# Block-sparse attention and a gated MLP on one core: chunk masks by product for the last four head pairs, and batch 0's query halves on GpSimd

## The chip, the cores and the metric

One core of a Trainium2 chip runs one program. The metric is device time of one execution in microseconds. A core has TensorE (PE; its weight loads are listed as PEld), VectorE (DVE), ScalarE (ACT), GpSimd (POOL) and SyncE (SP), each with an instruction queue of its own that is worked in order, and 16 DMA engines that the queues of SyncE and, for six loads at the start, ScalarE feed.

## What is computed

Attention with a selection of chunks, then a gated MLP. There are 4 batches, 8 heads, 768 positions, 64 elements per head; a chunk has 32 positions, so there are 24 of them.

```python
k_min, k_max = k_chunks.min(axis=3), k_chunks.max(axis=3)
ub = np.sum(np.maximum(q[:, :, :, None, :] * k_min[:, :, None, :, :],
                       q[:, :, :, None, :] * k_max[:, :, None, :, :]), axis=-1)
ub = np.where(causal, ub, -1e9)                      # by chunk
top_chunks = np.argsort(ub, axis=-1)[..., -6:]
scores = scale * q @ k.T
mask = sel & (pos[:, None] >= pos[None, :])          # chosen chunks, and causal
attn = softmax(np.where(mask, scores, -1e9))
x = (attn @ v)                                       # to [3072 tokens, 512]
h = x @ w_in                                         # 512 -> 2048
out = (h * np.clip(h + 3, 0, 6) / 6) @ w_out         # 2048 -> 512
```

The first six chunks of positions (192 rows of queries, `Q0`) select all that causality leaves them, so a mask is needed for the other 576 (`NQ`, twice `HQ` = 288) only.

## The kernel before

**Units of work.** Two heads of a batch are a *pair*; there are 16, and batch b has pairs 4b to 4b+3. The score matrix of a pair is kept transposed (keys on partitions, queries along the free dimension) and cut to its causal part in six *units* u (`UNITS`, line 23): blocks of up to 512 columns for both heads, 2688 columns per head in all. The MLP works on *groups* g of 384 tokens, two for each batch.

**The order is written by hand.** `ORDER` (line 34) is a list of tokens such as `S.12.4.a`: operation, pair and unit, PSUM place. The last lines (690 to 692) run down the list and issue each token's instructions to its engine. Within an engine the instructions stand in that order; between engines they wait for data and for buffers. PSUM has three double banks `a`, `b`, `c` (tiles PBa, PBb, PBc) and two single ones `x`, `y` (PSx, PSy).

What the tokens mean:

- `LK LQ LV AK AQ` load half a pair's K, Q, V for one head (SP, or ACT for the two with A); `lk lq lv` load pairs 4 to 15, K and Q turned in blocks of 32 by the access pattern, and `kd qd` finish the turning on DVE. `wl wc` load and cast weights.
- Batch 0 (pairs 0 to 3): `KT QT` transpose on PE in halves; `KB QB` cast to bf16 on ACT (lines 402, 405); `MX MN` chunk maxima and minima on DVE; `RP`, `RN` or `RA` the positive and negative part of Q (lines 419, 423, 427); `UH` the bounds on PE; `UB TH T8 SE LH MT` bias, transpose, top 8, comparison, transpose back and copy of the mask.
- Pairs 4 to 15: `mx mn kx rp` the same preparation; `ud us tr tm se tb` bounds of two pairs at once on PE (line 490), bias, 32x32 block transpose, top 8, comparison and transpose back on DVE (lines 495 to 512); `mv` copies the mask into spare rows of the query tile on POOL (line 314); `kc qc` cast K and Q (POOL, ACT).
- `S` scores on PE, `ex` exp on ACT into PT, `af` the causal triangle of a diagonal block on POOL (line 555). `A B` weighted values on PE, `na nb` division by the sum and storing to XB on DVE.
- XB is transposed for the MLP into XT by `X`/`xe` (PE, then a copy on DVE; lines 604, 608) or by `xt` (three DMA transposes on SP; line 597). `H` hidden matmuls (line 615, 1 token = 2x4 matmuls of 384 columns), `hu gt` the gate on ACT and DVE (lines 623, 626), `O` output projection (line 653, 4 matmuls of 512 columns a token), `ot st` scaling on ACT and the store on SP.

**Scores and masks before.** Pairs 0 to 3 score with both heads' 64 rows side by side in the array (line 537) and add a mask term by further matmuls (line 542). Pairs 4 to 15 (line 530) put 32 rows of mask and a fixed spreading matrix beside the 64 rows of K and Q in one matmul of 96 or 128 rows, so that a chunk that is not chosen gets -8192 before exp; the two heads follow one another.

## Time and profile before

| | |
|---|---|
| time, median of 3 runs | 270.98 us (270.34 to 271.39) |
| profiled execution | 270.87 us, span 268.9 us |
| DVE, ACT, POOL busy | 179.4, 184.1, 123.3 us |
| granted TensorE clock | 0.999 |
| DMA | 35.94 MB, mean 134 GB/s |
| longest waits, in total | POOL (`af`) for ACT's exp 50.0 us; DVE (`gt`) for ACT's `hu` 33.5 us |

The page gives busy time by engine, the chain of work that ended last, groups of instructions by source line, and DMA issues. The trace also gives each engine's instructions in order of time, merged where neighbours are alike, with the idle time ahead of them and what ended it in brackets. "96*128 96x384" of a matmul is the size of its weights and of the streamed operand.

### The profile page before, as it was taken

Reading aid. Unit: us, or ns where it says so; the run is one execution under the profiler, and the core shown is the slowest. Engines: PE = TensorE matmul, PEld = TensorE weight load, DVE = VectorE, ACT = ScalarE, POOL = GpSimd, SP = SyncE. Lnnn points to the kernel's source line nnn. Section 1 sums busy time; section 2 is a strip of 40 time slices with the busy share of each in tenths; the row PEclk is TensorE's granted clock in tenths of the full one; section 3 lists DMA queues with packets and bytes.
Section 4 is the critical chain, followed back from the end, with each engine's and each line's share of the span. In section 5 each row is a group of like instructions: output and inputs, shape, how many; then the busy total and the mean of one; then the engine's idle time right before and its main releaser. Section 6 shows DMA issues by size and latency. Waiting matters only on the chain.

```text
span 268.9 us, 6552 instructions
## 1 busy us (share of the span) xinstructions
PE 256.6 (95%) x2492; PEld 156.0 (58%) x2492; DVE 179.4 (67%) x430; ACT 184.1 (68%) x251; POOL 123.3 (46%) x234
## 2 busy tenths in 40 slices
PE   3998989999999999999999999999999999999995
PEld 1665777655455568655555655655555666555544
DVE  2698897889596889988897488746792314632420
ACT  1568899476689898494986588876668796423432
POOL 6901899676857895083392214850325521000000
PEclk9999999999999999999999999999999999999999
DMA  8979895789999928979667437512420021221023
GB/s 167 195 165 169 161 338 111 280 225 324 230 185 194 221 65 143 211 152 204 99 156 160 97 82 174 95 25 58 124 57 2 0 61 41 46 93 39 0 78 117
DMA packets 129102, 35.94 MB, mean 134 GB/s; under 512 B 121776, under 2 KB 122032, under 8 KB 129072
## 3 DMA queue, kind: packets, MB, share of 16 engines
q1 hardware_dynamic: 126672, 34.94, 56.7%
q10 hardware_dynamic: 2400, 0.59, 1.2%
q8 instruction: 19, 0.31, 0.5%
q14 instruction: 11, 0.09, 0.1%
HBM read 27.26 MB, written 6.29 MB: 125 GB/s over the span
## 4 chain that ended last, share of the span: by engine, by line
PE 78%; DVE 6%; ACT 6%; DMA 4%; SPq 2%; issue 2%; POOL 1%; DVEq 0%; ACTq 0%
PE PSx L653 15%; PE PBc L615 11%; PE PBb L615 9%; PE PSy L653 8%; PE PBa L615 8%; PE PBa L530 4%; PE PBb L530 3%; ACT PT L548 3%; PE PBc L530 3%; PE PBa L653 3%; PE PSy L571 2%; PE PSx L571 2%; DMA KSM<-in_k_dram 2%; DMA XT<-XB 2%; ACT U L623 1%
## 5 line engine op out<-in xcount | busy, mean ns | idle before, releaser
L615 PEld LDWEIGHTS <-WIN 128*128 128x128 bf16 x512 | 49.2, 98 | 34.6 <-issue 1.0
L555 POOL TENSOR_SCALAR_AFFINE_SELECT PT<-PT 128x256 bf16<-128x256 bf16 x96 | 37.2, 411 | 52.5 <-ACT PT L548 50.0
L653 PEld LDWEIGHTS <-GT 128*128 128x128 bf16 x368 | 34.7, 97 | 36.2 <-issue 1.5
L653 PE MATMUL PSx<-WOUT,GT 128*128 128x512 bf16 x208 | 51.4, 379 | 0.0
L615 PE MATMUL PBc<-XT,WIN 128*128 128x384 bf16 x200 | 36.6, 326 | 0.3 <-ACT PT L548 0.2
L548 ACT ACTIVATE PT<-PBa 128x1024 bf16<-128x1024 f32 (+2 forms) x35 | 32.2, 919 | 5.9 <-PE PBa L530 5.2
L548 ACT ACTIVATE PT<-PBb 128x1024 bf16<-128x1024 f32 (+2 forms) x32 | 29.3, 916 | 5.3 <-PE PBb L530 4.4
L626 DVE SCALAR_TENSOR_TENSOR GT<-U,PBc 128x768 bf16<-128x768 bf16 x25 | 23.6, 946 | 12.0 <-ACT U L623 11.8
L623 ACT ACTIVATE U<-PBc 128x768 bf16<-128x768 f32 x25 | 20.2, 809 | 16.0 <-PE PBc L615 14.5
L548 ACT ACTIVATE PT<-PBc 128x1024 bf16<-128x1024 f32 (+2 forms) x29 | 27.2, 937 | 5.3 <-PE PBc L530 4.6
L530 PEld LDWEIGHTS <-KB 96*128 96x128 bf16 x240 | 21.4, 98 | 15.5 <-issue 1.6
L615 PE MATMUL PBb<-XT,WIN 128*128 128x384 bf16 x160 | 29.3, 326 | 0.6 <-DMA XT<-XB 0.6
L653 PE MATMUL PSy<-WOUT,GT 128*128 128x512 bf16 x112 | 28.1, 379 | 0.0
L615 PE MATMUL PBa<-XT,WIN 128*128 128x384 bf16 x152 | 27.8, 326 | 0.0
L626 DVE SCALAR_TENSOR_TENSOR GT<-U,PBb 128x768 bf16<-128x768 bf16 x20 | 19.0, 950 | 11.3 <-ACT U L623 11.1
L314 POOL COPY QB<-MTM 32x288 bf16<-32x288 bf16 x48 | 20.2, 421 | 12.9 <-DVE MTM L512 8.3
L571 PEld LDWEIGHTS <-PT 128*128 128x128 bf16 x672 | 23.8, 97 | 3.0 <-issue 0.2
L626 DVE SCALAR_TENSOR_TENSOR GT<-U,PBa 128x768 bf16<-128x768 bf16 x19 | 18.0, 945 | 10.6 <-ACT U L623 10.6
L623 ACT ACTIVATE U<-PBa 128x768 bf16<-128x768 f32 x19 | 15.3, 807 | 13.5 <-PE PBa L615 13.5
L623 ACT ACTIVATE U<-PBb 128x768 bf16<-128x768 f32 x20 | 16.2, 810 | 12.2 <-PE PBb L615 12.0
L362 DVE TENSOR_REDUCE KM<-KSM 128x24 f32<-128x768 f32 x24 | 22.2, 942 | 0.2
L306 POOL CAST KB<-KSM 64x768 bf16<-64x768 f32 x24 | 19.7, 827 | 5.6 <-issue 3.1
(193 smaller groups left out, 385.3 us busy)
## 6 DMA issues: line engine op xcount, KB each, us to landing
out_dram<-OT SPq DMA_DIRECT2D x23, 256.0 KB, 2.4
...
WS<-in_moe_w_in_dram SPq DMA_DIRECT2D x4, 1024.0 KB, 7.7
WS<-in_moe_w_out_dram SPq DMA_DIRECT2D x4, 1024.0 KB, 6.2
...
```

The source lines that it names most:

```text
L306: engine.tensor_copy(T, src[i % 3][rows])
L314: nc.gpsimd.tensor_copy(aug(QB, i, e)[g:g + CH, Q0 + HQ * h:Q0 + HQ * (h + 1)], MTD[(d // 2) % 2][src:src + CH, e])
L362: nc.vector.tensor_reduce(out=KM[i % 4][:, m, 0:NCH], in_=k_turned(i).rearrange("p (c w) -> p c w", w=CH), axis=AX.X, op=(A.max, A.min)[m] ...
L530: nc.tensor.matmul(PSB[c][:, e, at:at + n], lhsT=K[rows, j * P:(j + 1) * P], rhs=Q[rows, q0:q0 + n], start=True, stop=True)
L548: nc.scalar.activation(PT[i % 3][u][:, :, 0:n], PSB[slot["S", i, u]][:, :, 0:n], ACT.Exp, scale=float(scale))
L555: nc.gpsimd.affine_select(out=T[:, :, lo:lo + P], in_=T[:, :, lo:lo + P], pattern=[[0, 2], [1, P]], compare_op=A.is_ge, fill=0.0, base=0, ...
L571: nc.tensor.matmul(O[:, e, t, :], lhsT=PT[i % 3][u][:, e, lo:lo + P], rhs=VB[i % 4][:, j, e, :], start=(j == 0), stop=(j == qb))
L615: nc.tensor.matmul(PSB[c][:, ff, 0:GRP], lhsT=WIN[:, kt, (2 * f + ff) * P:(2 * f + ff + 1) * P], rhs=XT[g % 3][:, kt, :], start=(kt == 0), ...
L623: nc.scalar.activation(slot["R", g, f][:], PSB[slot["H", g, f]][:, :, 0:GRP], ACT.Relu, bias=3.0)
L626: nc.vector.scalar_tensor_tensor(out=GT[g % 2][:, 2 * f:2 * f + 2, :], in0=slot["R", g, f][:], scalar=6.0, in1=PSB[slot["H", g, f]][:, :, ...
L653: nc.tensor.matmul(PSS[c], lhsT=GT[g % 2][:, f, t * P:(t + 1) * P], rhs=WOUT[:, f, :], start=(f == 0), stop=(f == FT - 1))
```

## The change

For pairs 12 to 15 (`PRODUCT`, the pairs with an `sm` token) the scores are made as in pairs 0 to 3, the two heads in two 64-row tiles, without a mask term. The comparison gives 1 for a chosen chunk. `sm` writes the mask of a pair to a DRAM tile, each of its 32 chunk rows four times; `ml` reads for one key block j the four chunks' rows back, each onto 32 partitions; `am` clears the triangle of the diagonal block in it, and `mu` multiplies PT by it behind exp. The masks lie in the weight staging tiles WS and in two new tiles MX5, which hold the identity and the spreading matrix of batch 0 earlier. `mv` falls away for these pairs, `kc` and `qc` cast all 128 rows at once, and `af` stays for the units of the first 192 queries alone.

For batch 0 ACT copies a half of Q once to SBUF (`QF`), and POOL makes the bf16 cast (`QC`) and the positive part (`PP`) from there, in place of ACT's `QB` and `RP`. Group 2 uses `xt` in place of `X` and `xe`. The whole list `ORDER` is another one. Number of tokens, before and after: `QB` 8 to 0, `RP` 8 to 0, `QF` `QC` `PP` 0 to 8 each; `X` `xe` 6 to 4 each, `xt` 5 to 6; `af` 80 to 68, `mv` 24 to 16, `kc` and `qc` 24 to 20 each; `sm` 0 to 4, `ml` `mu` 0 to 24 each, `am` 0 to 16; all others keep their number.

The list's first lines, and its lines from pair 12's bounds to the first hidden group of batch 3, then the functions:

```diff
+LK.0.1.0 AK.0.0.1 LQ.0.1.1 LQ.0.1.0 LK.0.0.0 PRP AK.1.0.1 LQ.0.0.0 LK.1.0.0 AQ.0.0.1 LK.2.0.0 LK.0.1.1 LQ.1.0.0 PRI
+AK.2.0.1 PRD Z.b.4 PRL EG.0 QT.0.1.y EG.2 KT.0.0.x MN.0.0 MX.0.0 KT.1.0.b MX.1.0 MN.1.0 QT.0.0.a RN.0.0 EG.3
+LK.1.1.1 KT.0.1.c AQ.2.0.1 LQ.2.0.0 AQ.1.0.1 KB.0.0 KT.2.0.x QF.0.1 PP.0.1 QC.0.1 LK.3.0.1 LK.1.1.0 QF.0.0 KB.1.0
+RA.0.1 PP.0.0 MX.2.0 UH.0.0.a MN.2.0 UB.0.0 LV.1.0.1 LK.3.0.0 QT.2.0.y TH.0.0.b LQ.1.1.0 QC.0.0 KB.2.0 MN.0.1
+LK.2.1.1 MX.0.1 EG.1 QF.2.0 T8.0.0 RN.2.0 LQ.1.1.1 QC.2.0 PP.2.0 QT.1.0.x QF.1.0 QC.1.0 PP.1.0 KB.0.1 UH.0.1.a
+UB.0.1 UH.2.0.c KT.3.0.y UB.2.0 SE.0.0 RN.1.0 KT.1.1.a KB.1.1 MX.3.0 LQ.3.0.0 LK.3.1.1 MN.3.0 TH.0.1.c T8.0.1
+LQ.2.1.1 QT.1.1.x LQ.3.0.1 UH.1.0.b UB.1.0 MN.1.1 QF.1.1 QC.1.1 PP.1.1 KB.3.0 LV.1.1.1 QT.3.0.y LQ.3.1.1 RA.1.1
+LH.0.0.x LQ.3.1.0 MT.0.0 S.0.1.b QF.3.0 LQ.2.1.0 LK.2.1.0 SE.0.1 S.0.0.c ex.0.1 ex.0.0 PP.3.0 LV.0.1.0 MX.1.1
...
+O.3.0.1.x O.3.0.2.x kc.13 S.12.1.a ex.12.1 vc.12 af.10.3 kx.13 qc.13 mn.14 ud.12.c lk.15 lq.15 qd.14 S.12.4.a
+ex.10.5 us.12 tr.12 tm.12.1 af.9.5 B.9.0.y B.9.1.y vc.13 ex.12.4 tm.12.0 S.11.3.c se.12 S.11.5.b af.10.5 ex.11.5
+O.3.0.3.x lv.14 S.11.4.a ot.3.0 tb.12 sm.12 ex.11.3 af.11.3 H.4.0.b ex.11.4 hu.4.0 gt.4.0 H.4.1.c hu.4.1 gt.4.1
+sm.13 H.4.5.a hu.4.5 gt.4.5 rp.14 ml.12.2 st.3.0 nb.9 ml.12.0 kd.15 B.10.0.x B.10.1.x nb.10 af.11.5 S.11.2.b qc.14
+mx.15 ex.11.2 af.11.2 vc.14 ml.13.0 H.4.2.c hu.4.2 gt.4.2 ml.13.5 H.4.3.a hu.4.3 gt.4.3 O.4.0.0.y H.4.7.b hu.4.7
+gt.4.7 ml.12.3 am.12.2 B.11.0.x qd.15 H.4.4.c hu.4.4 gt.4.4 ml.13.2 am.13.2 B.11.1.x nb.11 am.13.5 mn.15 kx.15
+ml.12.4 ml.13.4 rp.15 kx.14 O.4.0.1.y H.4.6.a hu.4.6 gt.4.6 S.13.4.b S.13.2.c kc.14 ex.13.2 O.4.1.0.x O.4.1.1.x
+am.13.4 S.13.0.c ud.14.a ex.13.4 xt.5 S.12.3.b us.14 tr.14 tm.14.0 tm.14.1 ex.13.0 mu.13.0 ex.12.3 S.13.1.c ex.13.1
+O.4.0.2.y ml.13.3 ml.12.5 ml.12.1 ml.13.1 O.4.1.2.x lv.15 se.14 tb.14 sm.15 S.12.0.a mu.13.2 S.12.5.b ex.12.5
+ex.12.0 mu.12.0 S.12.2.c ex.12.2 sm.14 af.12.0 am.12.3 O.4.1.3.x H.5.1.b hu.5.1 gt.5.1 mu.13.4 ml.15.0 kc.15 H.5.6.a
+H.5.4.c hu.5.6 gt.5.6 hu.5.4 gt.5.4 O.4.0.3.y ot.4.0 am.12.5 am.12.4 mu.12.4 mu.12.3 ml.14.2 am.13.3 af.13.1 ml.14.4
+H.5.3.b ot.4.1 hu.5.3 vc.15 H.5.0.a hu.5.0 gt.5.3 mu.12.5 gt.5.0 mu.12.1 ml.14.1 H.5.7.c H.5.2.b hu.5.7 gt.5.7
+H.5.5.a mu.12.2 st.4.0 ml.14.0 qc.15 hu.5.2 gt.5.2 O.5.0.0.y O.5.1.0.x S.14.0.c S.13.3.b hu.5.5 gt.5.5 ml.15.2
+af.12.1 ml.14.3 am.14.2 am.14.4 mu.13.1 ex.13.3 mu.13.3 S.15.1.a O.5.0.1.y O.5.0.2.y O.5.0.3.y A.12.b na.12 ml.15.1
+O.5.1.1.x O.5.1.2.x st.4.1 ot.5.0 S.15.0.b am.15.2 ml.14.5 ex.15.1 ex.14.0 mu.14.0 af.14.0 S.14.1.a ex.14.1 af.13.0
+mu.15.1 af.15.1 af.14.1 ex.15.0 af.15.0 ml.15.4 O.5.2.0.y ml.15.5 st.5.0 O.5.1.3.x ot.5.1 A.13.c na.13 mu.14.1
+mu.15.0 O.5.2.1.y S.14.3.a S.15.4.b S.13.5.c ex.14.3 mu.14.3 O.5.2.2.y A.15.x A.14.a ex.13.5 mu.13.5 na.15 na.14
+B.12.0.c O.5.2.3.y ot.5.2 B.12.1.c nb.12 ex.15.4 O.4.2.0.x S.15.3.a S.14.2.c ex.15.3 am.15.5 S.15.2.b ex.14.2
+ex.15.2 O.4.2.1.x xt.6 ml.15.3 B.13.0.y am.14.5 am.14.3 O.4.2.2.x S.15.5.a S.14.4.c S.14.5.b O.4.2.3.x ex.15.5
+B.13.1.y H.6.0.a mu.14.2 nb.13 am.15.4 mu.15.2 ot.4.2 ex.14.5 mu.14.5 H.6.1.b ex.14.4 hu.6.0 hu.6.1 mu.15.4 H.6.2.c
+mu.14.4 B.14.0.y B.14.1.y gt.6.0 H.6.3.a am.15.3 mu.15.5 gt.6.1 mu.15.3 H.6.5.b hu.6.3 O.6.2.0.x hu.6.2 gt.6.3
...
+    PRODUCT = sorted(named("sm"))
...
+    MX5 = ring(2, [P, 1856], BF16, "MX5") if PRODUCT else []
+    IDENT32 = MX5[1][:, 0:2 * P].bitcast(FP32) if PRODUCT else const.tile([P, P], FP32, name="IDENT32")[:]
+    IDENTB = MX5[1][:, 2 * P:3 * P] if PRODUCT else const.tile([P, P], BF16, name="IDENTB")[:]
     BIASM = const.tile([P, HQ], FP32, name="BIASM")
     BIASH = [BIASM[0:64, 0:96], BIASM[0:64, 96:288]]
-    EM = const.tile([P, NBLK, 2, P], BF16, name="EM")
+    EMT = MX5[0][:, 0:2 * NBLK * P] if PRODUCT else const.tile([P, 2 * NBLK * P], BF16, name="EM")[:]
+    EM = EMT.rearrange("p (j h c) -> p j h c", h=2, c=P)
+    FIRST = [max(0, P * j - Q0) for j in range(NBLK)]
+    AT = [0, 0, 1152, 2240, 3200, 1152]
+    MX = [[(MX5[n][:] if j in (0, 5) else WS[n][:].rearrange("p a b -> p (a b)").bitcast(BF16))
+           [:, AT[j] - FIRST[j]:AT[j] - FIRST[j] + 2 * NQ] for j in range(NBLK)] for n in range(2)] if PRODUCT else []
+    dram = ctx.enter_context(tc.tile_pool(name="dram", bufs=1, space=bass.MemoryType.DRAM))
+    REP = 4
+    SCR = {i: dram.tile([CH, REP, 2 * NQ], BF16, name=f"SCR{i}") for i in PRODUCT}
...
-        def issue(i, e):
-            rows = slice(e * D, (e + 1) * D)
+        def issue(i, e=None):
+            rows = slice(0, P) if e is None else slice(e * D, (e + 1) * D)
             dst, src = (KB, KF) if kind == "K" else (QB, QF)
-            T = aug(dst, i, e)[rows]
+            T = aug(dst, i, e or 0)[rows]
...
+    def q_keep(i, h):
+        nc.scalar.copy(QF[i % 3][:, SH * h:SH * (h + 1)], PSS[slot["QT", i, h]][:, 0:SH])
...
+    def q_half_pool(i, h):
+        nc.gpsimd.tensor_copy(QB[i][:, SH * h:SH * (h + 1)], QF[i % 3][:, SH * h:SH * (h + 1)])
...
+    def plus_half_pool(i, h):
+        dst, src = part_of(RP, i, h, kept=True)
+        nc.gpsimd.tensor_scalar(out=dst, in0=src, scalar1=1.0, scalar2=0.0, op0=A.mult, op1=A.max)
...
-                                op=A.is_lt)
+                                op=A.is_ge if i in PRODUCT else A.is_lt)
...
+    def mask_store(i):
+        for h in range(2):
+            for e in range(2):
+                g = CH * (2 * (i % 2) + h)
+                nc.sync.dma_start(SCR[i][:, :, NQ * e + HQ * h:NQ * e + HQ * (h + 1)],
+                                  MTD[(i // 2) % 2][g:g + CH, e].unsqueeze(1).to_broadcast([CH, REP, HQ]))
+
+    def mask_load(i, j):
+        src = SCR[i][4 * j:4 * j + 4].rearrange("c r n -> (c r) n")[:, FIRST[j]:]
+        nc.sync.dma_start(MX[i % 2][j][:, FIRST[j]:], src.unsqueeze(1).to_broadcast([16, 8, 2 * NQ - FIRST[j]]))
+
+    def mask_view(i, j, lo, hi):
+        return MX[i % 2][j].rearrange("p (e n) -> p e n", e=2)[:, :, lo - Q0:hi - Q0]
+
+    def mask_causal(i, j):
+        T = mask_view(i, j, j * P, j * P + P)
+        nc.gpsimd.affine_select(out=T, in_=T, pattern=[[0, 2], [1, P]], compare_op=A.is_ge, fill=0.0, base=0,
+                                channel_multiplier=-1)
+
+    def mask_apply(i, u):
+        for at, j, q0, n in UNITS[u]:
+            lo = max(q0, Q0)
+            T = PT[i % 3][u][:, :, at + lo - q0:at + n]
+            nc.vector.tensor_tensor(out=T, in0=T, in1=mask_view(i, j, lo, q0 + n), op=A.mult)
...
-                    K, Q = aug(KB, i, e), aug(QB, i, e)
-                    rows = slice(0, P if e else 96)
+                    x = 0 if i in PRODUCT else e
+                    K, Q = aug(KB, i, x), aug(QB, i, x)
+                    rows = slice(e * D, (e + 1) * D) if i in PRODUCT else slice(0, P if e else 96)
+                    at_rows = dict(tile_position=(e * D, 0)) if i in PRODUCT else {}
                     nc.tensor.matmul(PSB[c][:, e, at:at + n], lhsT=K[rows, j * P:(j + 1) * P], rhs=Q[rows, q0:q0 + n],
-                                     start=True, stop=True)
+                                     start=True, stop=True, **at_rows)
...
-            if q0 <= j * P < q0 + n:
+            if q0 <= j * P < q0 + n and not (i in PRODUCT and j * P >= Q0):
```

More of the change, by code (lines that the diff above doesn't have):

```diff
@@ L280, in prologue_late @@
     def prologue_late():
-        nc.vector.tensor_copy(IDENTB[:], IDENT32[:])
-        nc.vector.memset(EM[:], 0.0)
+        nc.vector.tensor_copy(IDENTB, IDENT32)
+        nc.vector.memset(EM, 0.0)
     def spread(g):
@@ L326, in transposes @@
         for j in range(NBLK):
-            nc.tensor.transpose(flat[:, j * P:(j + 1) * P], src[:, j].rearrange("p e d -> p (e d)"), IDENT32[:])
+            nc.tensor.transpose(flat[:, j * P:(j + 1) * P], src[:, j].rearrange("p e d -> p (e d)"), IDENT32)
     def cols(c, lo, hi):
@@ L427, in minus_half_act, with minus_half_pool @@
         nc.scalar.activation(dst, src, ACT.Relu, scale=-1.0)
+    def plus_half_pool(i, h):
+        dst, src = part_of(RP, i, h, kept=True)
+        nc.gpsimd.tensor_scalar(out=dst, in0=src, scalar1=1.0, scalar2=0.0, op0=A.mult, op1=A.max)
+    def minus_half_pool(i, h):
+        dst, src = part_of(RN, i, h, kept=True)
+        nc.gpsimd.tensor_scalar(out=dst, in0=src, scalar1=-1.0, scalar2=0.0, op0=A.mult, op1=A.max)
     def bounds_half(i, h, c):
@@ L604, in x_transpose @@
                 nc.tensor.transpose(bf16(c)[:, kk * GRP + t * P:kk * GRP + (t + 1) * P],
-                                    XB[b % 2][:, TPG * half + t, (2 * n + kk) * P:(2 * n + kk + 1) * P], IDENTB[:])
+                                    XB[b % 2][:, TPG * half + t, (2 * n + kk) * P:(2 * n + kk + 1) * P], IDENTB)
     def x_copy(g, n):
```

141 lines of the change are left out of this document (60 added, 81 removed).

## The prediction

> **What bounds the kernel now.** I read the page's shares and its chain first, then the engines' busy time window by window.
>
> ```profile
> span 268.9 us, 6552 instructions
> PE 256.6 (95%) x2492; PEld 156.0 (58%) x2492; DVE 179.4 (67%) x430; ACT 184.1 (68%) x251; POOL 123.3 (46%) x234
> ...
> PE 78%; DVE 6%; ACT 6%; DMA 4%; SPq 2%; issue 2%; POOL 1%; DVEq 0%; ACTq 0%
> ```
>
> ```profile
> 15.00:20.00 5.00, 4.42 (x73) 3.15 (x72) 4.97 (x24) 3.48 (x9) 0.51 (x1) 1.00 0.70 155
> 200.00:210.00 10.00, 10.00 (x81) 5.67 (x79) 3.22 (x5) 8.09 (x11) 6.95 (x15) 1.00 0.01 2
> ```
>
> TensorE is busy for 95% of the span and carries 78% of the chain. A window's row gives the busy time of PE, its weight loads, DVE, ACT and POOL in that order, then clock and DMA. From 200 to 210 us TensorE is busy all the time and VectorE 3.2 us of it; from 15 to 20 TensorE is busy for 4.42 of 5 and VectorE for 4.97. So there are two stages: a head, in which TensorE waits for others, VectorE above all, and a body of some 220 us, which lasts as long as TensorE's own queue. A busy share does not price a matmul, because matmuls overlap. The price is the distance between starts, in TensorE's order of time:
>
> ```profile
> 18.82 0.34 PE L537 MATMUL PBb<-QB,KB 64*128 64x384 bf16 x2 [0.18 <-DVE UBT L443]
> 18.99 0.34 PE L542 MATMUL PBb<-MTM,EM 64*128 64x192 bf16 x4
> ...
> 38.43 0.51 PE L604 MATMUL PSy<-IDENTB,XB 128*128 128x128 bf16 x6
> 38.87 0.34 PE L537 MATMUL PBb<-QB,KB 64*128 64x384 bf16 x2
> 39.05 0.33 PE L542 MATMUL PBb<-MTM,EM 64*128 64x192 bf16 x4
> 39.31 1.09 PE L571 MATMUL PSx<-VB,PT 128*128 128x65 bf16 x30
> ...
> 43.35 1.46 PE L615 MATMUL PBc<-XT,WIN 128*128 128x384 bf16 x8 [0.23 <-ACT PT L548]
> ...
> 217.82 0.61 PE L530 MATMUL PBc<-QB,KB 96*128 96x384 bf16 x4
> 218.27 1.89 PE L653 MATMUL PSx<-WOUT,GT 128*128 128x512 bf16 x8
> ```
>
> The last column before the bracket is a count, and the second number is the length of the merged group, tail included. At 217.82 a score unit of the old kind (four matmuls, 1024 columns) starts 0.45 us ahead of the projection behind it: 0.45 us per 1024 columns, with no gap between line 530 and line 653. The first hidden group starts at 43.35 (end of the head). The profiled execution took 270.87 us, 2.0 more than its span; the sum below is made against it, and it stands 0.1 us under the median of 270.98.
>
> **The scores of pairs 12 to 15.** A pair's six units have 2688 columns for each of two heads, 5376 in all. At 0.45 us per 1024 that is 2.36 us per pair, one head after the other. Two 64-row tiles side by side are in this trace already: line 537 does it for pairs 0 to 3. At 18.82 two matmuls of 384 columns take 0.17 us together (next start 18.99), where line 530 needs 0.34. So a pair costs 5376/768 x 0.17 = 1.19 us; line 542's mask matmuls, which pairs 0 to 3 add, are not added here, as the mask becomes a product. Saved: 4 x (2.36 - 1.19) = **4.7 us** of TensorE's queue. It is on the path, since the body is TensorE's queue.
>
> **What switching the array costs.** The same rows show gaps that belong to no wait. The six transposes at 38.43 have 768 columns, 0.34 us, so they are done at 38.77, and the 64-row scores behind them start at 38.87: 0.10. Line 542's four at 39.05 take 0.17, to 39.22, and the 128-row values start at 39.31: 0.09. I take **0.10 us for each switch** between a 64-row and a 128-row arrangement. [...] From the first product score to the end, the old order switches 4 times (into and out of line 490 for pairs 12 and 14). The new one bundles the 24 units into nine groups (`S.12.1 ud.12.c S.12.4`, `S.13.4 S.13.2`, ..., `S.15.5 S.14.4 S.14.5`): 18 switches, and 4 more where the bound matmuls with their own 32-column tiles stand inside a group. 18 more x 0.10 = **1.8 us lost**. [...]
>
> **Two transposes less.** `X.2.0` and `X.2.1` become `xt.2`, three DMA transposes: 2 x 0.34 = **0.7 us saved** on TensorE, and two copies on VectorE.
>
> ```profile
> L597 SPq DMA_TRANSPOSE XT<-XB x15: 1196/1257/1569, 111.7 to 233.8; - x15
> ...
> DMA to landing us min/median/max: 2.4/2.5/4.2
> ```
>
> `xt.2` stands behind `na.6` (0.7 us of VectorE). Two issues of 1.26 us ahead of the third and its landing (2.5 us median, 4.2 at most) make 5.7 to 7.4 us from the end of `A.6`; TensorE has 6.7 us of work (values, scores, bounds and two projection parts, by columns) from there to the first matmul that reads it. So it is hidden at the median, and costs 0.7 us at the worst. Behind it on SyncE stand two stores and the next pairs' loads.
>
> **The head.** ScalarE's casts `QB` and positive parts `RP` (16) become 8 copies `QF` to SBUF, and GpSimd makes both from there.
>
> ```profile
> 12.27 0.52 ACT L419 ACTIVATE RP<-PSx 128x384 f32<-128x384 f32 x1
> 12.65 0.51 ACT L405 CAST QB<-PSx 128x384 bf16<-128x384 f32 x1
> ...
> 19.48 1.02 ACT L548 ACTIVATE PT<-PBb 128x1024 bf16<-128x1024 f32 x1 [0.93 <-PE PBb L542]
> ```
>
> ```profile
> L626 DVE SCALAR_TENSOR_TENSOR GT<-U,PBc 128x768 bf16<-128x768 bf16 x25 | 23.6, 946 | 12.0 <-ACT U L623 11.8
> ...
> L391 POOL CAST VB<-VS 128x384 bf16<-128x384 f32 x8 | 4.0, 506 | 7.3 <-DMA VS<-in_v_dram 7.2
> ...
> L608 DVE COPY XT<-PSy 128x768 bf16<-128x768 bf16 x5 | 2.8, 552 | 0.3 <-PE PSy L604 0.3
> ```
>
> The first exp starts at 19.48. A half costs ScalarE 0.38 us (12.27 to 12.65). Behind the first exp stand 8 such halves in the old order (`QB`, `RP`, `RA`, `KB`) and 6 in the new: 2 x 0.38 = 0.75 us less in a stretch that ScalarE fills. The time of the first exp is set by VectorE: it has 11 half reductions, the minus parts and the first top-8s to do in either order, but starts about a microsecond earlier, as the transposes up to its first reduction ask for five loads, and those of the old order for nine. GpSimd's share is 8 casts of 0.51 us (L391 has the shape) and 8 positive parts, which the trace does not show: the cast of the same shape bounds them below (0.3 for 192 columns, 0.5 for 384), twice that above; I take the cast, the nearer row. That is some 7 us, and from 15 to 20 us GpSimd is busy for 0.51. But the first part of the chain is tighter: `UH.0.0` needs `PP.0.0` behind three `EG` copies, near 10.8 us, where the old `UH.0.0` started at about 11.2. I take 0.5 us for the earlier start and 0.75 for ScalarE, **1.25 us saved**; ends: 1 us lost (positive parts at twice the cast, in front of each `UH`) and 3 us saved (all 16 halves' time and the whole earlier start).
>
> **The products and the masks' journey.** Off TensorE the change adds 24 `mu` (40 VectorE products), 16 `am` on GpSimd in place of 12 `af`, 16 small stores and 24 loads on SyncE. It removes 16 mask copies and four K casts from GpSimd and four Q casts from ScalarE: all off the path here. No row shows a product of two 16-bit tiles in SBUF. Below stands L608, 768 bf16 in 0.55 us; above stands L626, 768 in 0.95. A pair has ten products (four of 768, two of 384, four of 256), 4 us at the lower and 6.6 at the upper end, 16 to 26 us in all. I take the lower: there, as here, both ends are 16 bits wide. [...] VectorE has room: 3.2 us busy of 10 in the window from 200.
>
> The masks go bounds, top-8, transpose, DRAM, SBUF, mask of the diagonal, product.
>
> ```profile
> 189.99 0.76 DVE L495 TENSOR_TENSOR UBM<-PBa,BIASM 128x576 f32<-128x576 f32 x1 [2.43 <-PE PBa L490]
> 190.79 0.78 DVE L499 STREAM_TRANSPOSE UBT<-UBM 128x576 f32<-128x576 f32 x1
> 191.60 1.77 DVE L504 MAX8 T8D<-UBT 128x8 f32<-128x32 f32 x18
> ...
> 195.20 0.75 DVE L507 TENSOR_TENSOR SELD<-UBT,T8D 128x576 bf16<-128x576 f32 x1
> ...
> 199.03 0.77 DVE L512 STREAM_TRANSPOSE MTM<-SELD 128x576 bf16<-128x576 bf16 x1
> ```
>
> ```profile
> out_dram<-OT SPq DMA_DIRECT2D x23, 256.0 KB, 2.4
> ...
> WS<-in_moe_w_out_dram SPq DMA_DIRECT2D x4, 1024.0 KB, 6.2
> ```
>
> VectorE's part is 0.76 + 0.78 + 1.77 + 0.75 + 0.77 = 4.8 us; the new order puts one product and no gating between its links. Store: eight issues of 0.5 us for two pairs and a landing as that of an output (2.4). Load: 295 KB, between an output (256 KB, 2.4) and a weight quarter (1024 KB, 6.2), so by the slope of the two 2.6 us, and 1.45 us apart if the queue is full. For pairs 14 and 15 that is 4.8 + 0.7 + 4 + 2.4 + 2.6 = 14.5 us behind `ud.14`; TensorE has 17 us of work, by its columns, from there to `S.14.0` (8 hidden groups, 6 projection parts, 5 score units), and about 10 more to `A.14`. Masks 12 and 13 have 4 us more of it. The loads wait in SyncE's queue for the product that frees their buffer; behind them stand `st.4.0`, `st.4.1`, `st.5.0` and `xt.6`, and three output buffers let ScalarE run on without the stores. Four joints have a microsecond or less to spare: `xt.2`, `xt.3`, `xt.6` (behind two products and `na.15`, `na.14`, before `H.6.0`) and `O.5.0.1`, whose `gt.5.2` stands behind seven products. The first three lose 0.7 to 1.3 us each where a transpose lands at 4.2 us. I add **0.9 us** for the four, one such landing; nothing to 3 us is the bound.
>
> **The sum:** 270.87 - 4.7 + 1.8 - 0.7 - 1.25 + 0.9 = 266.9, so **266.9 us**, 1.5% under the time before.
>
> **The rivals.** (a) *The masks land late, and it is slower.* 12 loads of up to 295 KB for pairs 14 and 15 share one queue, in order, each behind a buffer that a product frees. At the slope of the two DMA rows (200 GB/s) the eighth, which `mu.15.1` needs, lands about 2 us before `A.15` asks. At half that rate each load takes 2.9 instead of 1.45 us, the eighth is 12 us later, and `A.15` and the banks behind it stall some 9 us: about 276. It turns slower than before (over 272.3) at loads of 2.4 us, two thirds over my slope. For it: the slope comes from rows that are far from a load of 1152-element rows out of a small tensor. Against it: the old run moves nearly nothing there (DMA share 0.01 in the window from 200). Chance 0.12. (b) *Products at L626's rate.* Seven of them ahead of `gt.5.2` are 3.5 us later, and B.14 1 us: 266.9 + 4 = 270.9, the same. Chance 0.08. (c) *The head is not shorter,* GpSimd's parts reach `UH` late: + 1.25 and up to 1 lost, 268 to 269. Chance 0.12. (d) *The tiles do not run side by side* so that only the costs stay: 266.9 + 4.7 = 271.6. Line 537 speaks against it. Chance 0.03. (e) *The rewritten order fills the head better:* all 3 us, 264 to 265. Chance 0.13. My forecast, 265 to 268.5, has 0.52.
>
> **How the numbers follow.** About 0.5% (1.35 us) is what a measurement of this kernel can tell from no change, so faster means under 269.6 and slower over 272.3. Faster: the forecast, (e) and (c), 0.77, less 0.05 for several small waits at once. Same: (b), (d) and that 0.05, 0.16. Slower: (a), 0.12. The range leaves out (e)'s best and most of (a): 263.5 to 271.5.
>
> **What would show it.** Right: the scores of pairs 12 to 15 in pairs of equal starts, 0.22 us of TensorE's time for 1024 columns; gaps of 0.1 us at some 22 places behind 145 us; the first hidden group near 43 to 44 us; products of 768 columns near 0.55 us; no wait of TensorE for line 563's loads. Wrong: TensorE idle behind 180 us with MX or WS as releaser (a), products near 0.95 us (b), a first exp behind 20 us (c), score starts one after the other (d).

## The result and the profile after

| | before | after |
|---|---|---|
| time, median | 270.83 us (270.34 to 271.39, 4 runs) | 275.03 us (274.66 to 275.36, 4 runs) |
| ratio after / before, 95% | | 1.0154 (1.0129 to 1.0179) |
| profiled execution, span | 270.87, 268.9 us | 275.36, 273.6 us |
| first hidden group (H) starts | 43.35 us | 50.94 us |

The changed kernel is 1.5% slower; the forecast was 1.5% faster. Ratios here and below leave out runs more than 1.5% longer than the fastest of their kernel (one of old_head's four, which is its profiled one, and one of joint_first's twelve), so that they need not be the quotient of the medians. The page after, the lines that answer to those shown of before (the span, the busy time of each engine, the shares of the chain that ended last):

```profile
span 273.6 us, 6605 instructions
...
PE 254.6 (93%) x2456; PEld 151.7 (55%) x2480; DVE 194.9 (71%) x468; ACT 178.7 (65%) x239; POOL 126.3 (46%) x230
...
PE 67%; DVE 10%; SPq 6%; POOL 5%; issue 5%; DMA 3%; ACT 2%; POOLq 0%; DVEq 0%; ACTq 0%
```

TensorE does 2 us less, but carries 67% of the chain instead of 78%: the others took over some 30 us of it. Where, the windows say. First the kernel before, cut at its first hidden group, then the changed one, cut at its own (stretch, its length, then the busy time of PE, its weight loads, DVE, ACT and POOL, clock and DMA):

```profile
0.00:43.35 43.35, 35.09 (x560) 25.22 (x561) 32.90 (x124) 31.11 (x53) 27.28 (x59) 1.00 0.89 191
43.35:265.40 222.05, 221.19 (x1931) 130.74 (x1931) 146.46 (x307) 152.59 (x198) 96.02 (x176) 1.00 0.53 124
```

```profile
0.00:50.94 50.94, 39.82 (x611) 28.30 (x612) 34.68 (x127) 31.80 (x47) 42.59 (x80) 1.00 0.84 187
50.94:269.90 218.96, 214.58 (x1851) 123.36 (x1871) 160.24 (x342) 146.52 (x192) 83.68 (x151) 1.00 0.68 154
```

The body is 3.1 us shorter (222.05 to 218.96) and the head 7.6 us longer. Of the 7.6, TensorE idled 11.12 us in the head instead of 8.26: 2.9 us. It was busy 4.73 us longer. Of that, 1.7 us is work that the new order puts in front of the first hidden group (three more half values `B` at 0.46 us, one `X` at 0.34). The other 3.0 us is the same work, taking longer; two thirds of that is TensorE running slowly for longer, as is worked out under warm_plus. TensorE in the changed kernel, in order of time (line 410 is line 397 of before, the transposes; line 471 is line 437, the bounds):

```profile
10.26 0.90 PE L410 MATMUL PSx<-MX,KSM 128*128 128x128 f32 x3 [0.30 <-ACT KB L415]
13.57 0.54 PE L471 MATMUL PBa<-RP,KM 64*32 64x96 f32 x8 [2.41 <-POOL RP L457]
...
16.40 0.87 PE L471 MATMUL PBa<-RP,KM 64*32 64x192 f32 x8
...
18.47 0.88 PE L410 MATMUL PSy<-MX,KSM 128*128 128x128 f32 x3
19.17 0.51 PE L410 MATMUL PBa<-MX,KSM 128*128 128x128 f32 x3
...
31.09 0.53 PE L471 MATMUL PBb<-RP,KM 64*32 64x192 f32 x8 [1.17 <-POOL RP L457]
```

The first bounds (13.57) start 2.4 us later than before (11.20), after a wait for GpSimd's positive part. And the same three transposes take 0.88 us at 18.47 and 0.51 at 19.17: TensorE comes to its full rate at 18.9 us. In the kernel before that point lies at 12.4:

```profile
11.49 0.57 PE L437 MATMUL PBb<-WOUT,KM 64*32 64x96 f32 x8
...
12.13 0.40 PE L437 MATMUL PBc<-WOUT,KM 64*32 64x96 f32 x8
12.47 0.55 PE L397 MATMUL PBa<-IDENT,KSM 128*128 128x128 f32 x3
```

GpSimd's and ScalarE's own rows show what came late:

```profile
10.74 1.49 POOL L457 TENSOR_SCALAR RP<-QS 128x384 f32<-128x384 f32 x1 [1.30 <-issue]
12.19 0.50 POOL L427 CAST QB<-QS 128x384 bf16<-128x384 f32 x1
12.66 0.85 POOL L457 TENSOR_SCALAR RP<-QS 128x192 f32<-128x192 f32 x1
```

```profile
8.43 1.28 ACT L415 ACT_TABLE_LOAD   x1 [8.43 <-DVE KM L434]
9.72 0.48 ACT L415 CAST KB<-PSx 128x384 bf16<-128x384 f32 x1
10.10 0.48 ACT L421 COPY QS<-PSy 128x384 f32<-128x384 f32 x1
```

A positive part takes 1.49 us where the cast of the same 384 columns takes 0.50. The one that the first bounds need (12.66) stands behind one that they don't need and behind a cast, and all of it behind ScalarE's table load. The far end of the kernel looks as forecast. Line 591 is the scores of pairs 12 to 15, line 676 the hidden matmuls:

```profile
184.25 1.46 PE L676 MATMUL PBa<-XT,WIN 128*128 128x384 bf16 x8
185.64 0.39 PE L591 MATMUL PBb<-QB,KB 64*128 64x384 bf16 x4
185.87 0.38 PE L591 MATMUL PBc<-QB,KB 64*128 64x384 bf16 x4
186.19 1.04 PE L714 MATMUL PSx<-WOUT,GT 128*128 128x512 bf16 x4
```

From 185.64 to 185.87 are 0.23 us for a unit of 1024 columns, where it was 0.45; 185.87 + 0.23 leaves 0.09 us to 186.19, the switch of the array.

### The profile page after: what moved, and what is told of

It reads as the page before. It is cut to its first block, busy times and chain, and to the rows that moved or that the text cites. A ratio compares the mean times of both kernels' runs of the same rounds, so it can differ in the third digit from the quotient of the medians.

```text
span 273.6 us, 6605 instructions
## 1 busy us (share of the span) xinstructions
PE 254.6 (93%) x2456; PEld 151.7 (55%) x2480; DVE 194.9 (71%) x468; ACT 178.7 (65%) x239; POOL 126.3 (46%) x230
## 4 chain that ended last, share of the span: by engine, by line
PE 67%; DVE 10%; SPq 6%; POOL 5%; issue 5%; DMA 3%; ACT 2%; POOLq 0%; DVEq 0%; ACTq 0%
PE PSx L714 12%; PE PBb L676 10%; PE PBa L676 9%; PE PSy L714 8%; PE PBc L676 8%; SPq L399 4%; PE PBa L714 2%; PE PBb L591 2%; PE PBa L591 2%; PE PSy L632 2%; PE PBc L591 2%; DVE PT L577 2%; DVE GT L687 2%; SPq L231 1%; PE PSx L632 1%
## 5 line engine op out<-in xcount | busy, mean ns | idle before, releaser
L714 PE MATMUL PSx<-WOUT,GT 128*128 128x512 bf16 x163 | 42.0, 379 | 0.8 <-ACT OT L721 0.2
L616 POOL TENSOR_SCALAR_AFFINE_SELECT PT<-PT 128x256 bf16<-128x256 bf16 x80 | 30.9, 407 | 21.8 <-ACT PT L609 16.7
L676 PE MATMUL PBb<-XT,WIN 128*128 128x384 bf16 x184 | 33.8, 326 | 1.7 <-DVE XT L669 0.9
L714 PE MATMUL PSy<-WOUT,GT 128*128 128x512 bf16 x133 | 33.9, 379 | 0.9 <-issue 0.5
L684 ACT ACTIVATE U<-PBa 128x768 bf16<-128x768 f32 x22 | 17.8, 811 | 19.9 <-PE PBa L676 19.4
L684 ACT ACTIVATE U<-PBb 128x768 bf16<-128x768 f32 x23 | 18.7, 811 | 14.8 <-PE PBb L676 14.6
L676 PE MATMUL PBc<-XT,WIN 128*128 128x384 bf16 x152 | 27.8, 326 | 0.2 <-DMA XT<-XB 0.2
L591 PEld LDWEIGHTS <-KB 96*128 96x128 bf16 (+1 forms) x240 | 17.2, 97 | 16.3 <-issue 4.4
L684 ACT ACTIVATE U<-PBc 128x768 bf16<-128x768 f32 x19 | 15.4, 808 | 11.5 <-PE PBc L676 11.5
L327 POOL COPY QB<-MTM 32x288 bf16<-32x288 bf16 x32 | 13.4, 420 | 16.1 <-DVE MTM L546 14.8
L687 DVE SCALAR_TENSOR_TENSOR GT<-U,PBc 128x768 bf16<-128x768 bf16 x19 | 17.9, 944 | 3.2 <-ACT U L684 3.0
L335 POOL CAST VB<-VS 128x768 bf16<-128x768 f32 x12 | 10.2, 854 | 19.0 <-DMA VS<-in_v_dram 16.8
```

The lines of the kernel that those rows point to most:

```text
L327: nc.gpsimd.tensor_copy(aug(QB, i, e)[g:g + CH, Q0 + HQ * h:Q0 + HQ * (h + 1)], MTD[(d // 2) % 2][src:src + CH, e])
L335: nc.gpsimd.tensor_copy(VB[i % 4][:, :, :, 0:D], VS[i % 2][:].rearrange("p e j d -> p j e d"))
L591: nc.tensor.matmul(PSB[c][:, e, at:at + n], lhsT=K[rows, j * P:(j + 1) * P], rhs=Q[rows, q0:q0 + n], start=True, stop=True, **at_rows)
L616: nc.gpsimd.affine_select(out=T[:, :, lo:lo + P], in_=T[:, :, lo:lo + P], pattern=[[0, 2], [1, P]], compare_op=A.is_ge, fill=0.0, base=0, ...
L676: nc.tensor.matmul(PSB[c][:, ff, 0:GRP], lhsT=WIN[:, kt, (2 * f + ff) * P:(2 * f + ff + 1) * P], rhs=XT[g % 3][:, kt, :], start=(kt == 0), ...
L684: nc.scalar.activation(slot["R", g, f][:], PSB[slot["H", g, f]][:, :, 0:GRP], ACT.Relu, bias=3.0)
```

## The experiments

The kernel before ran again beside each group of experiments (medians 271.4 to 272.0 us there), so ratios to it are compared, not times. **Theory 1**: GpSimd's positive parts make the head late. **Theory 2**, its rival: the new order itself does. **Theory 3** came from the trace: TensorE's slow rate lasts longer because of the gaps.

**act_plus: the positive parts back on ScalarE.**

```diff
-    QF.i.h ... PP.i.h     (batch 0, eight times)
+    RP.i.h QF.i.h
```

> The changed kernel with batch 0's positive parts back on ScalarE (from PSUM, one ahead of each copy of Q); the casts of Q stay on GpSimd, the order is the changed one. Theory 1 (the positive parts on GpSimd, 1.49 us for 384 columns and 0.85 for 192, stand at the head of every chain of bounds and make the head late): the wait of L471 for GpSimd goes, the first hidden group falls from 50.9 to 46 to 48 us, the time from 275.0 to 270 to 272.5. Theory 2 (the new order of loads and stages in the head costs the time, whichever engine makes the positive part): 274 to 276, the first hidden group stays near 50.5.

Measured: 272.80 us, ratio 1.0034 (1.0001 to 1.0067); first hidden group at 48.20. So 1.2% of the 1.5% goes away with one operation moved back, and theory 2 falls for that part. The time missed its range by 0.3 us, with the kernel before 1.0 us higher than in the first runs; the first hidden group missed by 0.2 us, and the windows say why that much is left:

```profile
0.00:48.20 48.20, 39.85 (x612) 28.06 (x613) 34.86 (x127) 33.86 (x55) 33.76 (x72) 1.00 0.82 182
48.20:266.00 217.80, 215.82 (x1874) 123.41 (x1870) 159.51 (x342) 146.52 (x192) 84.44 (x151) 1.00 0.69 158
```

TensorE idles 8.35 us in this head, as much as before (8.26), but is busy as long as in the changed kernel (39.85): the slow stretch stays, to 17.1 us.

**act_all: the cast back on ScalarE too.**

```diff
-    QF.i.h ... PP.i.h ... QC.i.h
+    RP.i.h QB.i.h
```

> The changed kernel with batch 0's positive part and bf16 Q both made by ScalarE straight from PSUM, as before, in the changed order of everything else. Theory 1: GpSimd loses 9.4 us of positive parts and 4.0 of casts, so this is at least as fast as the run with the positive parts alone moved back, 269.5 to 272. Theory 2: 274 to 276.

Measured: 272.96 us, 1.0027 (0.9996 to 1.0057), no different from act_plus and 1 us above the range in us, among runs in which the kernel before was 1 us higher too. GpSimd's casts cost nothing that can be measured.

**plus_in_before: the positive parts on GpSimd in the kernel before.** `KEEP` is a part of GT that is free in the head, so no load has to wait for it.

```diff
     def plus_half(i, h):
         dst, src = part_of(RP, i, h)
-        nc.scalar.activation(dst, src, ACT.Relu)
+        KEEP = GT[0][:].rearrange("p a b -> p (a b)").bitcast(FP32)[:, S * i + SH * h:S * i + SH * (h + 1)]
+        nc.scalar.copy(KEEP, PSS[slot["QT", i, h]][:, 0:SH])
+        nc.gpsimd.tensor_scalar(out=dst, in0=KEEP[:, (Q0, 0)[h]:SH], scalar1=1.0, scalar2=0.0, op0=A.mult, op1=A.max)
```

> The kernel before, in its own order, with one thing changed: where ScalarE made batch 0's positive part from PSUM it copies the fp32 Q to a free buffer, and GpSimd makes the positive part from that copy in the changed kernel's form (1.49 us for 384 columns, 0.85 for 192 there). Theory 1: 9.4 us more on GpSimd and 1.5 to 2 us more in each chain of bounds ahead of its first product; PE waits for L437's operand, the first hidden group goes from 43.4 to 45.5 to 47.5, the ratio to before is 1.007 to 1.015. Theory 2 (only the new order suffers from it, before has room on GpSimd, which was busy 27 of its first 43 us): 0.999 to 1.004.

Measured: 278.50 us, 1.0271 (1.0247 to 1.0296), first hidden group at 50.6, first exp at 25.4 instead of 19.5. The direction is theory 1's; the size is twice what was expected. TensorE there, the two waits:

```profile
12.27 0.54 PE L439 MATMUL PBb<-RP,KM 64*32 64x96 f32 x8 [0.98 <-POOL RP L421]
...
21.93 0.78 PE L439 MATMUL PBb<-RP,KM 64*32 64x192 f32 x8 [3.14 <-POOL RP L421]
```

The second wait is the costly one: behind it TensorE was back at its slow rate (bounds 0.78 and 0.88 us instead of 0.53 and 0.51), and the trace's granted clock says so too: 0.54 from 22 to 23 us, 0.50 from 23 to 25.

**one_op: GpSimd's positive part in one operation.**

```diff
-        nc.gpsimd.tensor_scalar(out=dst, in0=src, scalar1=1.0, scalar2=0.0, op0=A.mult, op1=A.max)
+        nc.gpsimd.tensor_scalar(out=dst, in0=src, scalar1=0.0, scalar2=None, op0=A.max)
```

> The changed kernel with GpSimd's positive part as one operation (maximum with zero) instead of two (times one, then maximum with zero). If GpSimd's time goes by operations, 384 columns take 0.8 to 1.0 us instead of 1.49 and the time falls by 1 to 1.5 us, to 273.5 to 274.2; if it goes by the instruction's form, 1.4 to 1.5 us and the time stays at 275.

Its groups on GpSimd (the last numbers: busy us in all, mean ns of one):

```profile
L456 POOL TENSOR_SCALAR RP<-QS 128x384 f32<-128x384 f32 x4 | 4.7, 1167 | 1.3 <-issue 1.3
L456 POOL TENSOR_SCALAR RP<-QS 128x192 f32<-128x192 f32 x4 | 2.7, 685 | 0.1
```

Measured: 273.89 us, 1.0098 (1.0073 to 1.0124). Neither price was right: 1.17 us, between the two. The time followed, inside its range: 2 us less on GpSimd (9.4 to 7.4), 1.5 us less in ratio. Per column the two operations take (1492 - 849)/192 = 3.3 ns, one takes 2.5, and some 0.2 us are fixed.

**early_table: the table load at the start.**

```diff
-PRD ... S.11.1.b ... PRA
+PRD PRA
```

> The changed kernel with ScalarE's exponential of one small row put right behind VectorE's first fills, so that the table load of 1.28 us lies in the time before ScalarE's first cast (it stood at 8.43 us, ahead of that cast). Theory 1 in its second part (the table load is in the way of Q's first copy, for which GpSimd waited 1.30 us): GpSimd's first positive part starts at 9.5 instead of 10.7, the time falls by 0.8 to 1.3 us, to 273.7 to 274.2. Rival: GpSimd is the bound of the head over 20 us and the gain is lost behind it or behind the loads, 274.7 to 275.2.

Measured: 275.09 us, 1.0140 (1.0073 to 1.0207). GpSimd's first positive part started at 9.58 us as expected, and the first hidden group came 1.4 us earlier in its profile (49.5). The time settles nothing: the interval covers both sides. The table load is tested again below, in warm_plus beside warm_act.

**warm_after and warm_before: ten matmuls of zeros at the start instead of four,** in the changed kernel and in the kernel before.

```diff
-Z.b.4
+Z.b.10
```

> The changed kernel with ten instead of four matmuls of zeros at its start, so that TensorE is busy from 1.3 to 5.7 us, where it waited 2.56 us for the identity. In the changed kernel's trace three fp32 transposes take 0.85 to 0.90 us up to 18.5 us and 0.51 to 0.55 after it; before, the fall is at 12.4 us. Theory 3 (TensorE comes to its full rate only after a stretch of unbroken work, and the gaps in the new head put this off by six us): the fall comes at 6 to 10 us, the first hidden group at 48.5 to 50, the time at 272.5 to 274.2. Rival (the slow stretch only fills time in which the chain waits for GpSimd anyway): 274.7 to 275.3.

> The kernel before with ten instead of four matmuls of zeros at its start. Theory 3: its own slow stretch of 6.3 to 12.4 us shrinks too; some 18 transposes and 32 products of bounds lie there, 5.3 us of work that would take 3.2, so up to 2 us, less where loads end the waits: ratio 0.993 to 0.999. Rival (loads set the pace of those first us): ratio 0.999 to 1.001.

Measured: 275.34 us, 1.0117 (1.0080 to 1.0153), and 272.04 us, 1.0011 (0.9988 to 1.0035). In both, TensorE is at its full rate from the first transpose on (three of them in 0.55 us at 5.77, and in 0.52 at 6.34). In the changed kernel it doesn't last; TensorE in warm_after:

```profile
9.92 0.55 PE L409 MATMUL PSx<-MX,KSM 128*128 128x128 f32 x3 [0.19 <-ACT KB L414]
13.24 0.37 PE L470 MATMUL PBa<-RP,KM 64*32 64x96 f32 x8 [2.77 <-POOL RP L456]
13.70 0.55 PE L409 MATMUL PSy<-MX,QS 128*128 128x128 f32 x3
14.56 0.90 PE L409 MATMUL PSx<-MX,QS 128*128 128x128 f32 x3
...
18.05 0.49 PE L409 MATMUL PBa<-MX,KSM 128*128 128x128 f32 x3
```

After 2.77 us without work the transposes go back to 0.90 us, from 14.6 to 17.8. The granted clock falls with them: it is 0.50 from 15 to 17 us and 1.00 again from 18. On the page, which cuts the span into 40 equal slices and gives the clock of each in tenths (9 is 0.9 or more), the third slice, 13.7 to 20.5 us, stands out:

```profile
PEclk9979999999999999999999999999999999999999
```

So the wait for GpSimd costs twice: its own length, and the slow stretch behind it. What the ten matmuls are worth with that wait in place, the time can't tell: the first hidden group came at 49.8 us, inside theory 3's range, but the gain in ratio, from 1.0154 to 1.0117, lies within the two intervals, and 275.34 us is at the rival's edge, with the kernel before 0.9 us higher than in the first runs. In the kernel before, the first exp came a full microsecond earlier (18.53 instead of 19.48), and the time did not move. The rival holds there: loads end the waits later in that head. GpSimd's cast of V stands 1.63 us for its load, until 34.55, TensorE then 1.43 us for GpSimd, until 36.64, and the first hidden group starts at 44.21, 0.86 later than without the added matmuls.

**warm_act and warm_plus: both causes out.** warm_act is act_plus with ten matmuls of zeros; warm_plus has the early table load as well.

```diff
-Z.b.4 ... QF.i.h ... PP.i.h
+Z.b.10 ... RP.i.h QF.i.h
```

> The changed kernel with the positive parts on ScalarE and ten matmuls of zeros at the start, but ScalarE's table load left where it is (ahead of its first cast, at 8.4 us). It divides what the run with all three gained over the positive parts alone (from a ratio of 1.0034 to 0.997): if it is TensorE's rate, this run is at 0.996 to 0.999; if it is the table load, at 1.001 to 1.004, since ScalarE's first copy of Q then comes 1.3 us later and TensorE waits for it.

> The changed kernel with the positive parts on ScalarE, the table load at the start, and ten matmuls of zeros at the start: what stood in the way of the new head, one by one, is taken out together. If the gap in front of the first bounds is what lets TensorE fall back to its slow rate (the run with ten matmuls of zeros alone was at the fast rate until 14 us, then slow again to 17.5), the first hidden group is at 45.5 to 47 and the ratio to before 0.992 to 1.000. Rival (the issue of loads on SyncE paces the rest of the head): first hidden group at 47.5 to 48.2 as with the positive parts alone, ratio 1.001 to 1.006.

Measured: warm_act 271.08 us, 0.9976 (0.9955 to 0.9996); warm_plus 270.59 us, 0.9970 (0.9941 to 0.9999), first hidden group at 45.9 (47.0 in warm_act), in both no three transposes of the head over 0.58 us. From act_plus, TensorE's rate is worth 0.6% (1.6 us; the intervals just fail to touch), the table load nothing that can be told. While GpSimd's wait was there, the same ten matmuls gave 0.4%, which can't be told from nothing. That is theory 3, and together with theory 1 it accounts for all of the loss against the kernel before.

The profiles of warm_plus and warm_before also divide the 3.0 us by which the same work took longer in the head. Less what the six added matmuls of zeros take (2.3 and 1.9 us), TensorE is busy 36.3 us in warm_plus's head and 33.5 in warm_before's; with the slow stretches it was 39.8 and 35.1. So the slow rate costs 3.6 us in the changed kernel's head and 1.6 in the old one: 2.0 of the 3.0. The other 1.0 stays at the full rate too and belongs to the new order, which is what is left of theory 2.

**joint_first: a transposing load ahead of mask loads.** In warm_plus TensorE's longest wait behind the head is in front of group 5:

```profile
189.50 2.71 PE L674 MATMUL PBb<-XT,WIN 128*128 128x384 bf16 x8 [2.34 <-DMA XT<-XB]
192.01 1.92 PE L674 MATMUL PBa<-XT,WIN 128*128 128x384 bf16 x8
193.77 1.46 PE L674 MATMUL PBc<-XT,WIN 128*128 128x384 bf16 x8
```

This wait is paid twice as well: the two groups behind it take 2.71 and 1.92 us where 1.46 is usual, and the granted clock is 0.50 from 190 to 192 us. Nine of warm_plus's twelve runs have a mean granted clock of 0.999 or more (this one 0.994), so most did not pay the second part. Its data were ready when VectorE ended at 178.78 + 0.56 = 179.34, but SyncE issued four mask loads first:

```profile
178.42 2.52 SPq L561 DMA_DIRECT2D WS<-SCR  x4
181.05 3.87 SPq L656 DMA_TRANSPOSE XT<-XB  x3
```

```diff
-nb.11 am.13.5 mn.15 kx.15 ml.12.4 ml.13.4 ... ex.13.4 xt.5
+nb.11 xt.5 am.13.5 mn.15 kx.15 ml.12.4 ml.13.4 ... ex.13.4
```

> As the run with positive parts on ScalarE, early table load and ten matmuls of zeros, with the transposing loads of group 5 (three, 1.3 us of issue each) put on SyncE right behind the values that they take, ahead of four mask loads that were issued in 2.5 us before them; TensorE waited 2.34 us for their landing. If the queue's order made that wait, the wait falls by 1.5 to 2.3 us and the ratio to before is 0.988 to 0.994. Rival (the landing is slow because of what else the DMA engines move then, and the mask loads then come late instead): 0.995 to 1.000.

Measured: 270.36 us, 0.9949 (0.9918 to 0.9980). The wait is gone: group 5 starts at 190.10 without one and runs at 1.46 us, on a profile whose head was 1.8 us later. The landing got shorter too, 4.1 to 5.0 us from issue instead of 5.7 to 7.2 (2.5 is the median of all such loads in the kernel before), so the rival's part in the wait isn't excluded. In time the two ranges can't be told apart: beside warm_plus it is 0.2%, inside the intervals. New waits, for VectorE's gate, stand behind it:

```profile
196.74 1.46 PE L675 MATMUL PBa<-XT,WIN 128*128 128x384 bf16 x8 [0.35 <-DVE GT L686]
...
200.43 1.46 PE L675 MATMUL PBb<-XT,WIN 128*128 128x384 bf16 x8 [0.94 <-DVE GT L686]
```

This is the fastest version: 0.5% under the kernel before (0.2 to 0.8) and 2% under the changed one.

**old_head and old_head2: the old head in front of the new body.** The order of before up to its first hidden group (old_head) or its first six (old_head2), then the changed order for what is left; batch 0's halves as before.

```diff
-(the changed order's head)
+(the old order up to "ex.2.4", or up to "gt.0.5"; then the changed order less what is done)
```

> The order of before up to its first hidden group (positive part and bf16 Q on ScalarE), then the changed kernel's order for all that is left, with pairs 12 to 15 in 64-row tiles and masks as products. If all of the loss lies in the head: first hidden group at 44.5 to 45.5 (1.7 us of TensorE work is moved in front of it), 219 us from there to the end as in the changed kernel, 267 to 269.5. Rival: the 3.1 us that the changed kernel gained behind its first hidden group came from work made ready while TensorE stood idle in the head; then the rest grows and the time is 270 to 272.

> As the run with the old head, but the joint lies later: the order of before up to the first six hidden groups (TensorE stood idle 3.1 us at the earlier joint, for the values of pair 3), then the changed kernel's order for what is left. If the loss lies in the head alone, the first hidden group is at 43 to 44 us and the rest as in the changed kernel or up to 2 us longer for the joint: 267.5 to 270.5, ratio 0.987 to 0.997. Rival (the stretch behind the first hidden group is no shorter in the changed order, it only finds more work made ready): 271 to 273.

Measured: old_head 276.23 us, 1.0135 (1.0064 to 1.0207); old_head2 273.02 us, 1.0033 (1.0008 to 1.0059). old_head missed both of its ranges. Its profile, which is that of its longest run (278.35 us), shows a joint of my own: TensorE stood 3.1 us from 45.3 until GpSimd's cast of V for pair 3, and the windows around it show the granted clock falling to 0.58 and 0.56. How much of this the three shorter runs share, no profile shows.

```profile
46.00:50.00 4.00, 1.56 (x29) 1.66 (x30) 1.81 (x2) 2.58 (x4) 3.92 (x8) 0.58 0.60 176
50.00:54.00 4.00, 4.00 (x41) 2.60 (x39) 0.75 (x2) 0.83 (x2) 1.89 (x1) 0.56 0.97 364
```

old_head2 has the old head to the tenth (43.3), and lost all the same, at the upper end of its rival's range:

```profile
0.00:43.30 43.30, 34.98 (x561) 25.03 (x562) 32.78 (x124) 31.01 (x53) 26.42 (x58) 1.00 0.84 189
43.30:266.20 222.90, 216.83 (x1895) 125.25 (x1919) 161.91 (x345) 148.96 (x194) 87.89 (x157) 1.00 0.69 158
```

Its body does 4.4 us less on TensorE than that of before and idles 6.1 us instead of 0.9. So "the loss lies in the head alone" is refuted as I put it: the new body gives its gain back to small waits. How much of that is due to the joint where the two orders meet stays open.

**rows128: the tiles alone.**

```diff
-rows = slice(e * D, (e + 1) * D) if i in PRODUCT else slice(0, P if e else 96)
-at_rows = dict(tile_position=(e * D, 0)) if i in PRODUCT else {}
+rows = slice(0, P) if i in PRODUCT else slice(0, P if e else 96)
+at_rows = {}
```

> The changed kernel with the scores of pairs 12 to 15 as matmuls over all 128 rows, one head after the other (each then sums both heads, so that the output differs), everything else as it is. It measures the side by side tiles alone. The forecast's terms: 4.7 us saved by the tiles less 1.8 for the switches between the array's forms, so this run is 2.9 us slower than the changed kernel, 277 to 278.5. Rival (TensorE is not the bound of that stretch in the changed kernel, VectorE's products or the exponentials are): within 1 us of 275.

Measured: 278.01 us, 1.0215 (1.0176 to 1.0253). Beside the changed kernel that is 0.6% in ratio (1.7 us) and 3.0 us in the medians, with the kernel before 0.9 higher here; in the profiles the stretch behind the first hidden group is 222.1 us instead of 219.0, 3.1 more, and TensorE is busy 2.8 us longer in it. The tiles' gain less the switches is there, between 1.7 and 3.1 us where 2.9 were forecast.

**no_products: without VectorE's products.**

```diff
-mu.i.u     (24 tokens)
```

> The changed kernel without VectorE's products of pairs 12 to 15 (the weights there aren't masked by chunks, so that the output differs); the masks are still stored, loaded and cut. If VectorE's 18.5 us lie beside other work, as the forecast had it, 274.5 to 275.2; if the late stretch is bound by VectorE (products between exponentials and values, or gates delayed behind them), 272.5 to 274.

Measured: 276.73 us, 1.0217 (1.0180 to 1.0254). It isn't faster, so nothing shows the late stretch to be bound by the products; that it is 0.6% slower than with them neither side expected, and its cause wasn't found.

## Why the prediction was wrong, point by point

- **The step that failed: GpSimd's positive parts.** "The cast of the same shape bounds them below (0.3 for 192 columns, 0.5 for 384), twice that above; I take the cast, the nearer row." They took 0.85 and 1.49 us, three times the cast and outside the upper end, which had no row behind it: a conversion and a two-operation arithmetic of one shape are not near each other on GpSimd (0.50 and 1.49 us for 384 columns). 9.4 us instead of 3.2. Two of them, 2.34 us, stand in front of the first bounds, with a cast of 0.50 between them (1.49 + 0.50 + 0.85, from 10.74). Shown by act_plus (1.2% of the 1.5%), one_op and plus_in_before.
- **The step "near 10.8 us" for `UH.0.0`** came out at 13.57. Besides the price I had `PP.0.0` "behind three `EG` copies"; it stood behind `PP.0.1` and `QC.0.1` too, and behind ScalarE's table load, which the new order uncovers. Moving the load gave nothing that can be told (warm_plus beside warm_act; early_table's interval is too wide).
- **A term that the sum lacked: TensorE's rate.** The head's term priced ScalarE, VectorE and GpSimd and put TensorE's own time at no change. The gaps moved the point where the full rate begins from 12.4 to 18.9 us: some 2.0 us of the 7.6 (warm_plus and warm_before), and 0.6% when it is taken out (warm_act). Another 1.0 us, TensorE's longer time for the same work in the new order, was put at nothing too. The profile of before had it, in the transposes of 0.87 us at 6.28 and of 0.55 at 12.47, and I did not read it.
- **"1.25 us saved" by an earlier first exp** was 0.5 for an earlier first exp and 0.75 for less work on ScalarE behind it. VectorE's reductions did start earlier (7.33 instead of 9.39 us), but the chain then waited for GpSimd. The first exp doesn't set the end of the head: warm_before had it 0.95 us earlier for no gain, and warm_plus at 18.2 with the first hidden group at 45.9. So even without GpSimd's wait the 0.5 was nothing; the 0.75 no run shows by itself. Rival (c) named the mechanism (GpSimd reaching `UH` late) and a first exp behind 20 us as its sign (it came at 22.65), but priced it at 2.25 us at most. Head in sum: 7.1 us worse than forecast (7.6 against 1.7 of moved work less 1.25).
- **The scores' 4.7 us and the switches' 1.8: right** by the rows at 185.64. Their difference of 2.9 us agrees with rows128's profile (3.1); its ratio gives less (1.7). The switches to the bounds' 32-column tiles, priced alike, show the same: 188.02 + 0.23 leaves 0.09 us to the bounds at 188.34 (line 524), and 188.85 + 0.51 leaves 0.11 to the scores at 189.47.
- **Two transposes less: right.** TensorE waited 0.23 us for `xt.2`.
- **Products at L608's rate: right.** 0.54 to 0.60 us on average for 768 columns, 18.5 us in all where 16 were forecast, and off the path as far as no_products shows. That is 0.7 to 0.8 ns a column for bf16 on both sides; line 507 of the kernel before, with fp32 operands, takes 0.75 us for 576 columns, 1.3 ns a column. The groups of 768 columns (busy us in all, mean ns of one):

```profile
L577 DVE TENSOR_TENSOR PT<-PT,WS 128x768 bf16<-128x768 bf16 x12 | 7.1, 601 | 1.4 <-ACT PT L609 1.4
...
L577 DVE TENSOR_TENSOR PT<-PT,MX 128x768 bf16<-128x768 bf16 x4 | 2.2, 542 | 2.4 <-ACT PT L609 2.4
```

- **Masks in time: right.** No wait of TensorE for line 563's loads; VectorE waited 0.6 us for them and GpSimd, off the path, 25.7. Rival (a) did not happen.
- **The joints' 0.9 us: a term that was mis-sized.** TensorE idles 4.4 us behind its first hidden group (218.96 - 214.58) instead of 0.9: 3.5 more, where 0.9 more was forecast. They lie partly at joints that I had not listed: VectorE's copy of a transposed group (0.9 us, the longest), `xt.5` behind mask loads (0.56 us here, 1.15 in act_plus, 2.34 in warm_plus), and a gate behind VectorE (0.3). The forecast took 2.5 to 4.2 us from a transposing load's issue to its landing; those of `xt.5` took 5.4 to 6.1. TensorE's own work behind the first hidden group fell by 6.6 us, where 5.3 were forecast (4.7 - 1.8 + 0.7, and the 1.7 moved in front), which hides part of this. The forecast had VectorE with room, from the window at 200 of the old order (3.22 of 10); in the new order it is the busiest beside TensorE there:

```profile
200.00:210.00 10.00, 9.69 (x60) 5.06 (x60) 8.92 (x17) 5.88 (x8) 2.13 (x4) 1.00 0.78 224
```

In sum, the head is 7.1 us worse than forecast and the body 1.3 (3.1 us shorter, of which 1.7 is the work moved in front, where 2.7 + 1.7 were forecast): 8.4 of the 8.5 us between 275.36 and 266.9. By the runs, the ratio went from 1.0154 to 1.0034 (positive parts), 0.9976 (TensorE's rate), 0.9970 (table load), 0.9949 (one joint). The last two steps lie within the intervals. The forecast's 0.985 is another 1.0% (2.6 us) off; the 1.25 us that were not found in the head, the 1.0 us of the new order and the remaining waits are of that order, but no run divides them.
